# Linear attention with a gated feed-forward on one core: kv norm in three vector steps, q sums on ScalarE, k's block swap as a product, q0 in four pieces, leading products in K halves

## The chip, the core and the metric

The kernel runs on one core of one Trainium2 chip. The core has TensorE (PE, matrix products, results in PSUM), VectorE (DVE), ScalarE (ACT), GpSimd (POOL) and SyncE (SP, which here issues DMAs). The time is the device time of one execution in microseconds (us). Three executions of the kernel before gave 293.3 us (median; 292.95 to 293.79).

## The reference, cut to what matters

```python
def _attn_ref(q, k, v):                      # each (8, 8, 576, 64)
    q_s = np.exp(q - np.max(q, axis=-1, keepdims=True))
    q_s = q_s / (np.sum(q_s, axis=-1, keepdims=True) + 1e-09)
    k_s = np.exp(k - np.max(k, axis=2, keepdims=True))
    k_s = k_s / (np.sum(k_s, axis=2, keepdims=True) + 1e-09)
    kv = np.einsum('bhsd,bhse->bhde', k_s, v)
    return np.einsum('bhsd,bhde->bhse', q_s, kv)

x = attn_out.transpose(0, 2, 1, 3).reshape(4608, 512)
h = x @ w_in                                 # (512, 2048)
g = h * (1.0 / (1.0 + np.exp(-beta * h)))
out = g @ w_out                              # (2048, 512)
```

q is normalised along the 64 columns of a row, k along the 576 rows of a head. Inputs and output are float32; the kernel computes products in bfloat16 with float32 sums.

## The kernel before, in words

**Units.** The feed-forward works on 9 chunks of 512 tokens. Eight hold the first 512 tokens of a batch (8 of the 9 sub-rows i that a partition holds), and the chunk numbered 7 holds the last sub-row of all batches, the tails. The 2048 hidden columns are 16 blocks of 128. Unit n is chunk n // 16 and block n % 16, so there are 144 units. A unit goes through four operations, named in the order by letters:

- **h n** (`st1`, L510): four products over the K tiles of 128, into one PSUM bank hT of 128 x 512;
- **th n** (`tanh`, L524): ScalarE reads that bank and writes the tanh to SBUF;
- **g n** (`gate`, L533): VectorE computes (th + 1) * h from SBUF and that bank, so that h needs to be half of x @ w_in (the 2.0 in `kv_norm`);
- **o n** (`st2`, L554): four products of g with 128 rows of w_out into the four banks acc0 to acc3, which gather the 16 units of a chunk. After the sixteenth, `o_ev` copies each acc to SBUF (osb) and `store` writes it out.

**Rings.** PSUM has eight banks: four acc, and four tiles hT0 to hT3 that are dealt out in turn by `take` to h, but also to kv, x, xt and qtrt (below), to beta and to the fills. There are 8 buffers for g and 3 for th.

**Attention.** For batch b: `q_max` (VectorE, L226), `q_sub` (POOL, L238), `q_exp` (ScalarE, L243), `q_sum` and `q_rcp` (VectorE, L264, L271, L272), `q_norm` (POOL, L278), then a transpose qT: by DMA for b of 1 and more, by TensorE (`q_tr`, L298) with copies for batch 0. For k: `k_max` (VectorE, L315) gives maxima by blocks of 32 partitions; `k_small` (L332, L337, L340) reduces them, swaps neighbouring blocks of 32 partitions by four instructions of 32 x 8, and combines both with the sign turned; `k_rep` (L349) spreads the result, `k_sub` adds it (POOL or VectorE, L359), `k_exp` (L364) follows. `kv_mm` (L385) computes kv with the sum of k's exponentials as a 65th column, for two halves J of the heads; `kv_norm` (L400, L401, L403) divides by that column, five VectorE instructions a half. `x_mm` (L433) multiplies qT by kv into x, `x_ev` copies it to xT in SBUF; `xt_mm` (L466) does the same for the tails.

**Order.** The order of all operations is written out by name: the list FIRST (L17 to L69) up to batch 5, and after it by due times. Each engine runs its instructions in that order; waits between engines are set when the program is built, from the tiles that instructions read and write. Weights are loaded in 16 halves of 512 KB into four staging tiles and cast to bfloat16 on POOL, ScalarE or VectorE; a staging tile is loaded again after its cast. SP issues the loads in the order of the list, with at most eight on their way.

**The start.** Batch 0 is cut finer: q in sub-rows 0 to 3, 4 to 7 and 8, in two halves of heads; the first four units ("leading") in two halves of 256 tokens. `fill` (L644) runs products without use to keep TensorE occupied before there is work.

Of the kernel before, what the change touches and what calls it, by code (L numbers as in the profile page):

```python
# [13 lines left out]
EPS = 1e-9  # L14


FIRST = """  # L17
ld_q0_1, consts, ld_q0_0, ld_k0_0, ld_k0_1, ld_v0_0, ld_v0_1, ld_beta, ld_w0_0, ld_w0_1, ld_q1_1, ld_w2_0, ld_w1_0,
ld_w2_1, ld_q1_0, qmax_0_0_1, qmax_0_1_1, qmax_0_2_1, qsub_0_0_1, qsub_0_1_1, qmax_0_0_0, qsub_0_0_0, qexp_0_0_1,
qsum_0_0_1, qmax_0_1_0, qsub_0_2_1, qsub_0_1_0, kmax_0_0, qexp_0_1_1, qexp_0_0_0, vcast_0_0=pool, qsum_0_0_0,  # L20
kmax_0_1, qrcp_0_0, qnorm_0_0_0, qnorm_0_0_1, fill_0, qtr_0_0_0, fill_1, qtr_0_0_1, beta_tr, ksmall_0, krep_0_0,
krep_0_1, ksub_0_2, ksub_0_3, qexp_0_2_1, qexp_0_1_0, vcast_0_1, qtrev_0_0_0, kexp_0_2, cast_w0_1=pool, cast_w0_0,
ksub_0_1, ksub_0_0, qsum_0_1_0, qsum_0_1_1, qrcp_0_1, beta_ev, kexp_0_3, kexp_0_0, kexp_0_1, fill_2, kv_0_1,
qtrev_0_0_1, cast_w2_0=act, fill_3, kv_0_0, kvn_0_1, qnorm_0_1_1, ld_w1_1, ld_k1_0, ld_w4_0, ld_k1_1, ld_w4_1,
x_0_0_1, kvn_0_0, qnorm_0_1_0, x_0_0_0, qtr_0_1_1, qtr_0_1_0, ld_w3_0, xev_0_0_0, xev_0_0_1=act, h_0_0, h_3_0,
ld_w6_0, qtrev_0_1_1, th_0_0, qmax_1_2, qmax_1_3, qtrev_0_1_0=dve, qmax_0_2_0, qsum_0_2_1, g_0_0, x_0_1_1, x_0_1_0,
cast_w1_0=pool, qsub_0_2_0, cast_w2_1=pool, h_1_0, h_2_0, qexp_0_2_0, xev_0_1_0=dve, qsum_0_2_0, qrcp_0_2, qmax_1_1,
xev_0_1_1=act, h_0_1, th_1_0, th_3_0, th_0_1, h_1_1, h_2_1, h_3_1, g_0_1, th_1_1, g_1_0, g_1_1, qmax_1_0, qnorm_0_2_1,
qnorm_0_2_0, qsub_1_1, th_2_1, th_3_1, th_2_0, ld_w6_1, cast_w1_1=pool, qsub_1_0, cast_w4_1=pool, cast_w3_0, ld_w3_1,
ld_w5_0, ld_w7_0, ld_w5_1, ld_k2_0, ld_v1_0, ld_v1_1, ld_k2_1, h_4, th_4, kmax_1_0, kmax_1_1, g_2_0, g_2_1, g_4,  # L30
qexp_1_2, qexp_1_3, cast_w4_0, o_0_0, o_0_1, o_1_1, h_5, o_1_0, o_2_0, th_5, h_7, h_6, kmax_1_2, g_3_0, g_3_1,
kmax_1_3, o_3_0, g_5, h_8, o_2_1, o_3_1, o_4, h_9, qexp_1_1, qexp_1_0, th_7, th_6, ksmall_1, g_6, h_11, cast_w6_0,
th_8, krep_1, g_7, g_8, qsum_1_1, qsum_1_0, cast_w6_1, th_9, g_9, cast_w3_1=act, h_12, h_10, th_11, cast_w5_0,
ksub_1_0, qrcp_1_0, ld_w7_1, qnorm_1_0, qsum_1_2, qsum_1_3, g_11, qrcp_1_1, ksub_1_1=dve, qnorm_1_1, qT_1, ld_q2_1,
kexp_1_0, kexp_1_1, cast_w7_0, cast_w5_1=act, th_10, th_12, g_10, o_5, o_6, o_7, o_8, o_9, h_14, h_13, o_10, h_15,
kexp_1_2, kexp_1_3, th_14, th_13, vcast_1_0, vcast_1_1, cast_w7_1=pool, kmax_2_1, g_12, kmax_2_0, o_11, o_12, th_15,
g_14, g_13, g_15, kmax_2_2, kv_1_0, kv_1_1, o_13, o_14, kvn_1_0, kvn_1_1, kmax_2_3, x_1_0, xev_1_0, x_1_1, xev_1_1,
o_15, xev_1_2, xev_1_3=act, ksmall_2, qmax_2_3, qmax_2_2, h_16_0, h_16_1, h_28, h_17_0, h_17_1, oev_0_2, th_16,
oev_0_3=act, oev_0_1=act, th_17, oev_0_0, ld_q2_0, ld_v2_1, ld_k3_1, ld_v3_1, g_16, krep_2, qmax_2_0, st_0_0, ld_q3_1,
ld_v2_0, qsub_2_1, h_20, h_18, g_17, th_18, qmax_2_1, g_18, th_20, qexp_2_2, qexp_2_3, g_20, ksub_2_1, qsub_2_0,  # L40
vcast_2_1, ksub_2_0, vcast_2_0, qsum_2_2, kmax_3_2, o_16, h_24, o_17, h_21, kexp_2_2, th_21, g_21, h_19, th_19, g_19,
o_18, h_23, o_19, h_22, o_20, o_21, qexp_2_1, th_24, th_23, qexp_2_0, th_22, qsum_2_1, qmax_3_2, g_23, g_24, g_22,
qtrt_0, qsum_2_0, qsum_2_3, qrcp_2_0, qrcp_2_1, h_25, kexp_2_1, kexp_2_0, qtrtev_0_1, th_25, g_25, o_22, o_23, h_27,
kexp_2_3, th_28, th_27, h_26, o_24, o_25, qtrtev_0_0=dve, qmax_3_3, g_28, g_27, th_26, g_26, xt_0, kv_2_0, kv_2_1,
qnorm_2_0, qnorm_2_1, st_0_3, ld_k3_0, ld_q4_1, ld_q3_0, ld_v3_0, ld_k4_1, st_0_2, qT_2, ld_q4_0, ld_k4_0, qsub_3_1,
xtev_0_0, xtev_0_1, h_30, o_26, h_29, o_27, o_28, qexp_3_3, qexp_3_2, th_29, th_30, qmax_3_0, qmax_3_1, kmax_3_1,
kmax_3_3, kvn_2_0, kvn_2_1, qsum_3_3, g_29, x_2_0, xev_2_0, o_29, x_2_1, xev_2_1, xev_2_2, xev_2_3, h_31, th_31, h_32,
h_40, qsub_3_0, th_32, qsum_3_2, kmax_3_0, g_30, ksmall_3, krep_3, g_31, qmax_4_2, g_32, h_34, h_44, h_37, qexp_3_1,
th_34, g_34, th_37, qrcp_3_1, kmax_4_1, h_33, o_30, o_31, g_37, th_33, g_33, vcast_3_1=act, oev_1_0, oev_1_2, oev_1_3,
ld_q5_1, ld_v4_1, st_0_1, oev_1_1, kmax_4_2, h_36, th_36, g_36, h_35, o_32, o_33, qnorm_3_1, ksub_3_1, th_40, th_35,  # L50
g_40, kmax_4_3, g_35, qexp_3_0, qsum_3_1, o_34, h_39, th_39, g_39, h_38, th_38, g_38, qsum_3_0, qrcp_3_0, kmax_4_0,
h_42, h_41, ksub_3_0, vcast_3_0, kexp_3_1, kexp_3_3, th_41, h_43, o_35, o_36, o_37, o_38, st_1_0, st_1_1, ld_q5_0,
st_1_2, qnorm_3_0, g_41, th_42, th_43, th_44, g_42, g_44, g_43, ksmall_4, xt_1, krep_4, xtev_1_0=dve, h_46, h_45,
kexp_3_0, kexp_3_2, xtev_1_1, th_46, th_45, qmax_4_3, ksub_4_0, st_1_3, qT_3, ld_v4_0, ld_k5_0, ld_k5_1, qsub_4_1,
ksub_4_1, kexp_4_0, o_39, kv_3_0, kv_3_1, o_40, o_41, g_45, g_46, kvn_3_0, kvn_3_1, x_3_0, xev_3_0=dve, x_3_1, o_42,
xev_3_2, xev_3_1=dve, xev_3_3, h_48, th_48, h_49, qexp_4_3, qmax_4_1, g_48, qmax_4_0, qsub_4_0, vcast_4_1, h_51, h_52,
o_43, o_44, h_53, th_51, th_49, g_49, qexp_4_2, g_51, th_52, g_52, qsum_4_3, h_54, xt_3, th_54, o_45, xtev_3_0,
xtev_3_1, h_47, h_55, qexp_4_0, th_47, vcast_4_0=dve, g_47, th_55, kexp_4_1, o_46, o_47, g_54, kexp_4_2, g_55, h_50,
xt_2, oev_2_2, oev_2_0, xtev_2_1, th_50, oev_2_3, oev_2_1, o_48, st_2_1, g_50, qsum_4_2, o_49, st_2_2, h_56, th_53,
xtev_2_0, st_2_0, h_57, g_53, qrcp_4_1, th_56, qexp_4_1, o_50, st_2_3, th_57, g_56, qsum_4_0, qsum_4_1, o_51, ld_v5_0,  # L60
kexp_4_3, o_52, ld_v5_1, g_57, o_53, o_54, h_58, qmax_5_0, qrcp_4_0, qnorm_4_0=dve, qnorm_4_1, qmax_5_1, qT_4, o_55,
th_58, qsub_5_0, g_58, kv_4_0, h_59, kvn_4_0, qmax_5_2, o_56, th_59, qexp_5_0, g_59, kv_4_1, h_60, kvn_4_1, qmax_5_3,
o_57, th_60, qsub_5_1, g_60, x_4_0, xev_4_0, h_61, qsum_5_0, xev_4_1, o_58, qexp_5_1, x_4_1, th_61, h_62, xev_4_2,
g_61, xev_4_3, o_59, qsum_5_1, qexp_5_2, h_63, qrcp_5_0, th_62, qnorm_5_0, o_60, qexp_5_3, g_62, th_63, qsum_5_2,
h_64, g_63, o_61, th_64, qsum_5_3, h_65, qrcp_5_1, g_64, o_62, qnorm_5_1, th_65, kmax_5_0, h_66, g_65, o_63, kmax_5_1,
oev_3_0, vcast_5_0, qT_5, h_67, oev_3_2, oev_3_1, st_3_0, th_66, vcast_5_1, oev_3_3, o_64, th_67, g_66, st_3_1, h_68,
kmax_5_2, st_3_2, o_65, th_68, g_67, h_69, kmax_5_3, st_3_3, g_68, o_66, th_69, ld_q6_0, ksmall_5, h_70, ld_q6_1,
krep_5, g_69, ksub_5_0
"""  # L69
PLAN = {}  # L70
for _i, _t in enumerate(FIRST.replace("_", " ").split(",")):
    _n, _, _e = _t.strip().partition("=")
    PLAN[_n] = (_i - 10000, _e or None)


@with_exitstack
def kernel(
# [20 lines left out]
    NR = 4  # L98
    LAST = 8
    LAG = 3  # L100
    NG = 8
    TAILS = 7
    NCH = 9


    ops = []

    def at(when, name, fn, eng=None):
        if name in PLAN:
            when, eng = PLAN[name][0], PLAN[name][1] or eng  # L110
        ops.append((when, len(ops), name, fn if eng is None else lambda: fn(ENGINES[eng])))

    ENGINES = {"act": nc.scalar, "dve": nc.vector, "pool": nc.gpsimd}
# [8 lines left out]
    ident = sbt("ident", [P, P], BF16)  # L122
    warm = sbt("warm", [P, P], BF16)
    beta_rows = sbt("beta_rows", [NJ, P], F32)
# [15 lines left out]
    kneg = sbt("kneg", [P, KT, 2], F32)  # L140
# [5 lines left out]
    xT = [sbt(f"xT{i}", [P, KT, 512], BF16) for i in range(2)]  # L146
    xTt = sbt("xTt", [P, KT, 512], BF16)
    g = [sbt(f"g{i}", [P, 512], BF16) for i in range(NG)]
    th = [sbt(f"th{i}", [P, 512], BF16) for i in range(3)]
    osb = sbt("osb", [P, 4, 512], F32)  # L150

    ring = [ps.tile([P, 512], F32, name=f"hT{i}") for i in range(NR)]
    acc = [ps.tile([P, 512], F32, name=f"acc{i}") for i in range(4)]
    place = {}
    done = set()
    turns = [(f"free{i}", ring[i]) for i in range(NR)]
    done.update(w for w, _ in turns)

    def take(*who):

        assert sum(last in done for last, _ in turns) >= len(who)
        for w in who:
            n = next(n for n, (last, _) in enumerate(turns) if last in done)
# [86 lines left out]
    def zs_of(b):  # L250
        if b:
            return qz[:]
# [590 lines left out]
```

## Time and profile before

| what | value |
|---|---|
| median of three runs | 293.3 us |
| span of the profiled execution | 291.8 us |
| TensorE busy | 273.9 us (94%) |
| VectorE, ScalarE, GpSimd busy | 207.3, 173.2, 127.5 us |
| h products into hT (L510) of 128 x 512 | 379 ns each by the row, 0.865 us for four in a row |
| th, 128 x 512 (L524) | 689 ns x 140 |
| g, 128 x 512 (L533) | 680 ns x 140 |
| first h starts | 19.88 us |
| last product ends | 287.4 us |
| q, k or v load, 576 KB, issue to landing | 5.0, 7.1, 8.3 us (median) |

The profiled execution's own time isn't listed beside its span; the median of the runs lies 1.5 us above that span. A group's duration runs from the issue of an instruction to its end, and products overlap, so a row of them takes less than the sum of their durations: the distance from start to start counts. "Idle before" is the time that an engine stood still ahead of an instruction, with what ended it.

### The profile page before, as it was taken

The numbers are of one execution on the slowest core, as the hardware profiler recorded it, in microseconds if no ns is written. First come the engines' busy times: TensorE is split into PE (matmuls) and PEld (weight loads), VectorE is DVE, ScalarE is ACT, GpSimd is POOL, SyncE is SP. The second block draws the span as 40 slices with busy tenths as digits, with TensorE's granted clock in tenths as the row PEclk, the third lists the DMA queues.
The fourth block names the chain that finished last, engine by engine and source line by source line (L and its number), as shares of the span: only waits on it lengthen the run. The fifth ranks groups of instructions, "written<-read, shape, count | busy, mean of one in ns | idle before, by whom it ended". The sixth has DMA issues, their size and how long they took to land.

```text
span 291.8 us, 5151 instructions
## 1 busy us (share of the span) xinstructions
PE 273.9 (94%) x1891; PEld 124.2 (43%) x1922; DVE 207.3 (71%) x446; ACT 173.2 (59%) x292; POOL 127.5 (44%) x85
## 2 busy tenths in 40 slices
PE   0888999999999999999999999999999999999993
PEld 0345344444344444444444444444444444444441
DVE  3988999989978875897976798578834353345350
ACT  2588794985677656727537854775575454444450
POOL 4898485698347583233835373547350000000000
PEclk9999999999999999999999999999999999999999
DMA  7999999998956570392199109920900060006005
GB/s 263 383 393 388 379 388 227 391 350 291 232 211 148 148 258 1 91 244 56 38 212 396 67 12 223 372 109 0 222 5 3 0 142 4 0 0 145 2 12 131
DMA packets 39577, 50.61 MB, mean 173 GB/s; under 512 B 18544, under 2 KB 18560, under 8 KB 39552
## 3 DMA queue, kind: packets, MB, share of 16 engines
q1 hardware_dynamic: 39472, 50.15, 56.0%
q8 instruction: 15, 0.25, 0.4%
q10 hardware_dynamic: 80, 0.13, 0.1%
q14 instruction: 10, 0.08, 0.1%
HBM read 36.71 MB, written 9.44 MB: 158 GB/s over the span
## 4 chain that ended last, share of the span: by engine, by line
PE 79%; DMA 9%; DVE 3%; issue 3%; POOL 2%; ACT 1%; SPq 0%
PE hT L510 38%; PE acc L554 37%; DMA wst<-in_moe_w_in_dram 4%; DMA qT<-qn 4%; PE hT L433 2%; DMA qf<-in_q_dram 1%; PE hT L385 1%; POOL w_in_b L184 1%; ACT th L524 1%; DVE km L315 1%; DVE g L533 1%; POOL qf L238 1%; POOL kf L359 0%; PE hT L466 0%; DVE acc L264 0%
## 5 line engine op out<-in xcount | busy, mean ns | idle before, releaser
L554 PE MATMUL acc<-w_out_b,g 128*128 128x512 bf16 x567 | 141.6, 379 | 1.2 <-DVE osb L184 0.4
L533 DVE SCALAR_TENSOR_TENSOR g<-th,hT 128x512 bf16<-128x512 bf16 (+1 forms) x148 | 97.1, 665 | 63.0 <-ACT th L524 62.1
L524 ACT ACTIVATE th<-hT,beta_c 128x512 bf16<-128x512 f32 (+1 forms) x148 | 98.2, 677 | 71.6 <-PE hT L510 66.8
L510 PE MATMUL hT<-xT,w_in_b 128*128 128x512 bf16 (+1 forms) x508 | 124.8, 373 | 2.1 <-DVE g L533 0.7
L554 PEld LDWEIGHTS <-g 128*128 128x128 bf16 x576 | 55.6, 98 | 68.6 <-issue 1.9
L510 PEld LDWEIGHTS <-w_in_b 128*128 128x128 bf16 x592 | 55.8, 98 | 65.5 <-issue 4.0
L278 POOL TENSOR_TENSOR qn<-eq,qz 128x1152 bf16<-128x1152 bf16 (+2 forms) x19 | 33.5, 1770 | 37.7 <-DVE qz L272 33.2
L238 POOL TENSOR_TENSOR qf<-qf,qm 128x1152 f32<-128x1152 f32 (+2 forms) x20 | 34.4, 1732 | 26.8 <-DVE qm L226 20.4
L359 POOL TENSOR_TENSOR kf<-kf,kmb 128x1152 f32<-128x1152 f32 (+1 forms) x14 | 35.3, 2538 | 17.1 <-DVE kmb L349 17.1
L226 DVE TENSOR_REDUCE qm<-qf 128x9 f32<-128x576 f32 (+2 forms) x34 | 23.7, 708 | 5.8 <-DMA qf<-in_q_dram 5.7
L364 ACT ACTIVATE ek<-kf 128x576 bf16<-128x576 f32 x32 | 21.1, 683 | 7.7 <-POOL kf L359 7.7
L315 DVE TRANSPOSE_TENSOR_REDUCE km<-kf 128x18 f32<-128x576 f32 (+1 forms) x30 | 23.9, 802 | 0.5 <-DMA kf<-in_k_dram 0.5
L243 ACT ACTIVATE eq<-qf 128x576 bf16<-128x576 f32 (+2 forms) x34 | 21.8, 655 | 3.0 <-POOL qf L238 2.9
L264 DVE TENSOR_REDUCE qz<-eq 128x9 f32<-128x576 bf16 (+1 forms) x30 | 21.0, 712 | 0.0
L182 ACT CAST xT<-hT 128x512 bf16<-128x512 f32 x25 | 13.4, 589 | 9.1 <-PE hT L433 9.1
L182 ACT COPY osb<-acc 128x512 f32<-128x512 f32 x20 | 10.9, 590 | 12.1 <-PE acc L554 12.1
L510 PE MATMUL hT<-xTt,w_in_b 128*128 128x512 bf16 x62 | 16.2, 379 | 0.1
L184 POOL CAST va<-vf 128x1152 bf16<-128x1152 f32 x13 | 14.7, 1149 | 0.8 <-DMA vf<-in_v_dram 0.8
L644 PE MATMUL hT<-eq,warm 128*128 128x512 bf16 x23 | 7.5, 476 | 7.3 <-ACT eq L243 7.3
L184 DVE COPY osb<-acc 128x512 f32<-128x512 f32 x16 | 10.4, 687 | 5.3 <-PE acc L554 5.1
L385 PEld LDWEIGHTS <-ek 64*64 64x64 bf16 x576 | 6.0, 107 | 5.5 <-issue 2.5
L385 PE MATMUL hT<-va,ek 64*64 64x65 bf16 x576 | 7.6, 194 | 0.2 <-ACT ek L364 0.2
(55 smaller groups left out, 91.0 us busy)
## 6 DMA issues: line engine op xcount, KB each, us to landing
qf<-in_q_dram SPq DMA_DIRECT2D x16, 576.0 KB, 5.0
kf<-in_k_dram SPq DMA_DIRECT2D x16, 576.0 KB, 7.1
vf<-in_v_dram SPq DMA_DIRECT2D x16, 576.0 KB, 8.3
out_dram<-osb SPq DMA_DIRECT2D x71, 128.0 KB, 2.4
wst<-in_moe_w_in_dram SPq DMA_DIRECT2D x8, 512.0 KB, 10.5
wst<-in_moe_w_out_dram SPq DMA_DIRECT2D x8, 512.0 KB, 10.6
out_dram<-osb ACTq DMA_DIRECT2D x1, 128.0 KB, 2.6
qT<-qn SPq DMA_TRANSPOSE x7, 3.9
```

The source lines that it names most:

```text
L182: act.copy(dst, src)
L184: eng.tensor_copy(dst, src)
L226: dve.tensor_reduce(qm[:, j : j + n, i0:i1], qf[b % 2][:, j : j + n, i0:i1], axis=AX.X, op=ALU.max)
L238: eng.tensor_tensor(x, x, m, ALU.subtract)
L243: act.activation(eq[:, i0:i1, j : j + n, :].rearrange("p i j d -> p j i d"), qf[b % 2][:, j : j + n, i0:i1], ACTF.Exp,)
L278: eng.tensor_tensor(qn[b % 2][:, i0:i1, j : j + n, :], eq[:, i0:i1, j : j + n, :], z, ALU.mult)
L315: dve.tensor_reduce(km[:, j : j + n].rearrange("p j i e -> p (j i e)"), kf[b % 2][:, j : j + n].rearrange("p j i (e c) -> p (j i e) c", c=32),
L359: eng.tensor_tensor(x, x, m, ALU.add)
L510: pe.matmul(place[("h", n)][:, cols(h)], w_in_b[:, kt, u * P : (u + 1) * P], x[:, kt, cols(h)], start=(kt == 0), stop=(kt == KT - 1),)
L524: act.activation(th[n % 3][:, cols(h)], place[("h", n)][:, cols(h)], ACTF.Tanh, scale=beta_c[:, u : u + 1])
L533: dve.scalar_tensor_tensor(out=g[n % NG][:, cols(h)], in0=th[n % 3][:, cols(h)], scalar=1.0, in1=place[("h", n)][:, cols(h)], op0=ALU.add, ...
L554: pe.matmul(acc[t][:], g[n % NG][:, t * P : (t + 1) * P], w_out_b[:, u, :], start=(u == 0), stop=(u == NJ - 1),)
```

## The change

- **kv norm**: three VectorE instructions (add and double, reciprocal, multiply) over both banks, and for batches 1 to 7 over both halves J at once, after the second half of kv. To reach two banks in one instruction, the four tiles hT0 to hT3 become one tile hT of 128 x 4 x 512; `take_pair` gives kv two of its banks, and the halves lie 128 columns apart.
- **First q sums**: for batch 0, sub-rows 0 to 3, the exponential is done in 8 ScalarE instructions of 128 x 64 a half, each with its sum as a second output into acc2, in place of one instruction of 128 x 512 and a VectorE sum.
- **k's maximum**: for batch 0 the swap of blocks is one product with a permutation matrix, into a bank of hT; for others the four 32 x 8 copies stay. The maximum is kept with its own sign and subtracted.
- **eps** is added from a tile in `q_rcp`.
- **q0** is loaded in four pieces: sub-rows 0 to 3 and 4 to 8 of each half of heads.
- **Leading products**: each half unit's four K tiles are two operations, tiles 0 and 2, then 1 and 3.
- The constants eps and swap are made on POOL; the last copy of acc3 is shared between ScalarE and VectorE; the whole order is written out in one list ORDER, with the same operations in the same places, save that kv's norm of batches 4 to 7 stands after the second half and the new operations (kred, kswap) after beta's transpose.

```diff
-    ring = [ps.tile([P, 512], F32, name=f"hT{i}") for i in range(NR)]
+    ring = ps.tile([P, NR, 512], F32, name="hT")
...
     def take(*who):
         for w in who:
             n = next(n for n, (last, _) in enumerate(turns) if last in done)
+            i = turns.pop(n)[1]
+            place[w] = ring[:, i, :]
+            turns.append((w, i))
+    def take_pair(w):
+        free = [n for n, (last, _) in enumerate(turns) if last in done][:2]
+        a, b = sorted(turns[n][1] for n in free)
+        place[w] = ring[:, a : b + 1 : b - a, :]
...
-        for s in range(2):
-            dve.tensor_scalar(kz[:, s, J : J + 1], w[s][:, D : D + 1], EPS, 2.0, op0=ALU.add, op1=ALU.mult)
-        dve.reciprocal(kz[:, :, J], kz[:, :, J])
-        for s in range(2):
-            dve.tensor_tensor(kvn[b % 2][:, J, s, :], w[s][:, 0:D], ..., ALU.mult)
+        w = place[key][:, :, P * J0 : P * (J0 + n)].rearrange("p s (J c) -> p J s c", J=n)
+        dve.tensor_scalar(z, w[:, :, :, D], EPS, 2.0, op0=ALU.add, op1=ALU.mult)
+        dve.reciprocal(z, z)
+        dve.tensor_tensor(kvn[b % 2][:, J0 : J0 + n], w[:, :, :, 0:D], ..., ALU.mult)
...
+    def q_exp_sum(b, j, n, i0, i1):
+        for a in range(j, j + n):
+            for i in range(i0, i1):
+                act.activation(eq[:, i, a, :], qf[b % 2][:, a, i, :], ACTF.Exp,
+                    accum_out=acc[2][:, KT * i + a : KT * i + a + 1])
...
+    def k_swap(b):
+        take(("swap", b))
+        pe.matmul(place[("swap", b)][:, 0 : 2 * KT], swap[:],
+            kmr[:].rearrange("p j e -> p (j e)"), start=True, stop=True)
...
+    def k_small(b):
+        if b:
+            for a in range(4):
+                o = kmr[32 * (a ^ 1) : 32 * (a ^ 1) + 32]
+                dve.tensor_tensor(kms[32 * a : 32 * a + 32], o, o, ALU.max)
+        dve.tensor_tensor(kmx[:], kmr[:], other, ALU.max)
...
+    for J in range(2):
+        for h, (i0, i1) in enumerate(((0, 4), (4, NI))):
+            op(f"ld q0 {J} {h}", lambda J=J, i0=i0, i1=i1: load_q(0, 2 * J, i0, i1))
...
+            for h in range(2):
+                for x in range(2):
+                    op(f"h {n} {h} {x}", lambda n=n, h=h, x=x: st1(n, (x, x + 2), h))
...
+        if (c, t) == (NCH - 1, 3):
+            act.copy(osb[:, t, 0:256], acc[t][:, 0:256])
+            dve.tensor_copy(osb[:, t, 256:512], acc[t][:, 256:512])
```

## The prediction, as put on record before the result

> **What bounds the kernel now.** I read the page's busy shares first.
>
> ```profile
> span 291.8 us, 5151 instructions
> PE 273.9 (94%) x1891; PEld 124.2 (43%) x1922; DVE 207.3 (71%) x446; ACT 173.2 (59%) x292; POOL 127.5 (44%) x85
> ```
>
> TensorE is busy 94% of the span, so what it does and waits for sets the time. Next come its own waits in the view of waits, longest first:
>
> ```profile
> PE hT L644 <- ACT eq L243: 7.3, 1, 7.3
> PE acc L298 <- POOL qn L278: 1.1, 2, 1.0
> PE hT L510 <- DVE g L533: 0.7, 1, 0.7
> PE acc L554 <- DVE osb L184: 0.4, 1, 0.4
> PE hT L433 <- DMA qT<-qn: 0.4, 1, 0.4
> ```
>
> After the first 7.3 us nothing is over 1.1 us. Once the first products run, TensorE goes through almost without a gap to 287.4 us. Why it can is seen in the timeline of one unit late in the run (columns: start us, length us, engine, line, operation, operands, count, idle before):
>
> ```profile
> 243.00 1.03 PE L510 MATMUL hT<-xTt,w_in_b 128*128 128x512 bf16 x4
> 243.06 0.69 DVE L533 SCALAR_TENSOR_TENSOR g<-th,hT 128x512 bf16<-128x512 bf16 x1 [1.04 <-ACT th L524]
> 243.87 1.03 PE L554 MATMUL acc<-w_out_b,g 128*128 128x512 bf16 x4
> 244.07 0.69 ACT L524 ACTIVATE th<-hT,beta_c 128x512 bf16<-128x512 f32 x1 [1.04 <-PE hT L510]
> ...
> 244.73 1.03 PE L510 MATMUL hT<-xTt,w_in_b 128*128 128x512 bf16 x4
> 244.78 0.69 DVE L533 SCALAR_TENSOR_TENSOR g<-th,hT 128x512 bf16<-128x512 bf16 x1 [1.04 <-ACT th L524]
> ```
>
> A unit is h (four products into one bank of hT), th (ScalarE reads it), g (VectorE reads it), and an o of an older unit. h begins at 243.00, o at 243.87, the next h at 244.73: 0.865 us each, 1.73 a unit. The next h starts while g of the unit before has only just begun (244.78) and will end at 245.47. That overlap is the kernel's whole economy: four tiles, so h of unit n+1 waits for g of unit n-3.
>
> **The ring as one tile.** The change makes the four tiles hT0 to hT3 one tile of four banks, so that one VectorE instruction can reach two banks. Waits are placed when the program is built, so I compared the built instruction lists with their waits. In the changed one, h of unit 64 writes bank 3 and waits for g of unit 63, which reads bank 0; th of a later unit waits for a g of another bank; the copy of beta (bank 2) waits for the swap product (bank 3), and the third fill (bank 0) for the readers of both. In the list of before, h waits for the last reader of its own tile. So in the changed program all of hT is handed over as one thing: every access by one engine waits for the last access by another, in the order of the list.
>
> The price of a plain unit (h, its th, its g, then the next h) by rows: four products 0.86; from h's end to th's start 244.07 - 243.865 = 0.21, say 0.22 (a waited-for h at 25.16 gave its th at 26.27, 1.11 in all); th 0.69; 0.03 (244.76 to 244.78); g 0.68; and 0.05 from a g's end to a waiting product (g starts 24.70 and takes 0.41, the product starts 25.16). Sum 2.53 against 1.73: the o (0.86) fits into the 1.67 in which the others read, but 0.8 us of every unit is idle.
>
> Over the whole order I went through the list of operations and cut it into rounds: writes of hT by TensorE, then reads, until the next write. From the first h there are 137 rounds, and 63 are the plain form. Added up:
> - TensorE writing: 140 h x 0.864 = 121.0; the four leading units in halves 3.5; kv 7 x 1.4 (0.68 to 0.7 a pair); x 14 x 0.45; tails and the late transposes 2.6: 143.2. Second products o that stand between two writes of one round: 19.5. Together 162.7.
> - Reading, with a handover 0.22 + 0.05 a round, 0.03 per change of reader, 0.07 less for two reads in a row on one engine: 140 th x 0.69, 140 g x 0.68, halves 6.8, xev 28 x 0.6, xtev 16 x 0.26, kv norm 7 x 0.75: 259.7.
> - o's longer than the reads that cover them: 2.4.
> That is 424.8 us from the first h to the last. Before, the same stretch ran from 19.88 to 280.3, 260.4 us.
>
> In some rounds a reader stands on its engine behind other work that the cover (about 1.8 us a round) can't hold: a reciprocal step, two sums and four kexp or cast instructions between th of unit 11 and th of unit 10 (about 4.5), sums and the swap of k between the g of units 30 to 32 (1.6), between g 56 and 57 (1.5), before g 58 (1.5), smaller ones 4.4; and at five later chunk ends ScalarE's two copies of acc stand ahead of th, waiting for that chunk's last o (1.35 each, 6.8). Estimate 20 us; bounds 0 and 45 (if nothing hides, twice my list).
>
> **The start.** Q0 in four pieces: the first piece is 256 of 576 KB; at the 390 GB/s of the page's DMA row that is 0.84 us less than the 3.97 us to the first maximum. POOL's three new constants (rows 0.10, 0.20, 0.29) end before 3 us and are hidden by that transfer. Two more DMA issues (0.48 each) delay the queue behind by 1 us, but w0 still waits for landings. First sums on ScalarE: 16 instructions of 128x64 replace two of 128x512 (0.63) and two VectorE sums (0.69). The trace has none with a sum; a 128x16 copy took 0.16, the 128x128 exp 0.30, and each waits for the one before (0.03), so eight take 1.5 to 2.6; I take 2.2, nearer to the 0.30 row. ScalarE then has the sums at about 10.8, just as kmax ends (11.66 less the two sums), and POOL's v cast (to 11.90) holds the norm anyway: it gains 0.25 us there.
>
> The block swap: kms and kneg (12.13 to 13.03) go, and a product comes. But it stands on TensorE behind the transposes of both first qn halves:
>
> ```profile
> 13.06 0.39 DVE L349 STREAM_TRANSPOSE acc<-kneg 128x192 f32<-128x192 f32 x1
> ...
> 14.26 0.40 PE L298 MATMUL acc<-ident,qn 128*128 128x128 bf16 x4 [0.18 <-POOL qn L278]
> 14.59 0.23 PE L628 MATMUL hT<-ident_f,beta_rows 16*128 16x16 f32 x1
> ```
>
> The swap can't start before 14.8 - 0.25, takes about the 0.23 of the beta product, then max 0.15: krep at 15.1 instead of 13.06. Behind it wait VectorE's three ksub (2.08), ksub 3 and two weight casts on POOL, kexp and kv. So the first h comes at 19.88 + 1.7 = 21.6 (bounds: 0 if other waits of kv cover it, and 3).
>
> **Small parts.** kv norm for b of 1 to 7 becomes 3 steps (0.15 + 0.17 + about 0.4) for 10 (4 x 0.15 + 2 x 0.17 + 4 x 0.22 = 1.8); before, TensorE's own work hid it, now 0.75 stands in the sum. Adding eps by a tensor is one instruction for one. K halves: the same products in the order 0, 2, 1, 3; both xT copies are done before the first th, so I take nothing (bounds -0.6, one copy, and 0). The last copy is split over two engines: 0.59 becomes about 0.4, -0.2.
>
> **Sum.** 21.6 + 424.8 = 446.4; the last 32 o's 32 x 0.216 + 0.2 = 7.1: 453.5; the tail 291.8 - 287.4 - 0.2 = 4.2: 457.7; queues 20: 478. The median of the runs (293.3) lies 1.5 over the profiled span, so the time is **479 us**.
>
> **Rivals.**
> 1. *The clock.* TensorE falls idle 1.67 us in most rounds less an o, and up to 3.7 in some.
>
> ```profile
> 7.26 5.03 PE L644 MATMUL hT<-eq,warm 128*128 128x512 bf16 x14 [7.26 <-ACT eq L243]
> ```
>
> After 7.26 us without work the 128x512 product took 0.36 instead of 0.216, though the granted clock stands at full. If gaps keep it there, 162.7 grows by 0.67 of itself (109) and the last o's by 4.6: 592; half the time so, 535. Against it: at 20 to 25 us products kept 0.12 per 256 columns with gaps of 0.2 to 0.7. The Trainium skill (TensorE: Matmul & The Clock Gate, "What's actually happening") says the clock halves after an idle window of some 3.4 us and returns after a busy one; the 0.36 row agrees in kind. By it only two or three rounds here would pay, some 5 us in all.
> 2. *Queues cost nothing, or ScalarE and VectorE read different banks side by side.* The 20 us vanish, or foreign th and g overlap in the grouped rounds (some 25 us by the same rows): 454 to 459. The built waits speak against the second.
> 3. *Not slower.* h of unit n+1 does not in truth wait for g of unit n, the four banks turn as before, and only start and tail move. The start's +1.7 is absorbed in the idle that TensorE has from 20 to 32 us (0.22, 0.73, 0.30) because the weights whose cast ends at 32.09 land at 30.99 either way: 293.3 + 1.7 - 1.25 - 0.2 = 293.5. It decides where the next h starts: at g's beginning (244.73 against 244.78) or after its end (245.47). The Trainium skill (PSUM — Partial Sum Buffer, "PSUM bank collisions raise a hardware error") keeps engines apart only within one bank, so by it the chip needs no such wait, and the time would be this 293.5. Nothing in before's trace contradicts it, as it overlaps banks; but a wait in the program is obeyed whether the chip needs it or not.
>
> **Chances.** Forecast (460 to 510) 0.73; clock 0.12; 2: 0.12; 3: 0.03. The range 450 to 540 leaves out the third and most of the clock's case. A measurement of this kernel can tell about 0.3% (0.9 us) from no change: faster 0.01, same 0.02, slower 0.97.
>
> **What would show it.** TensorE near 57% busy; its longest wait by far h <- DVE g, some 0.8 us about a hundred times; h every 2.53 us late in the run; ScalarE's idle before th ended by PE, not g. krep near 15. An h that starts before g of the unit before has ended proves me wrong; products of 0.36 show the clock.

## The result, and the profile after

The changed kernel takes 508.7 us (median of four runs, 507.1 to 515.9) against 293.1 for the kernel before: 1.733 times as long, 95% interval 1.729 to 1.737. Here and below, medians are over all executions and ratios over those within 1.5% of the kernel's fastest. The forecast was 479, range 450 to 540. The page of the profiled execution begins so (busy us, share of the span, instructions; below it a row with the granted TensorE clock in tenths, 40 slices):

```profile
span 506.9 us, 5168 instructions
PE 330.9 (65%) x1924; PEld 134.8 (27%) x1924; DVE 203.2 (40%) x388; ACT 177.8 (35%) x322; POOL 128.0 (25%) x88
...
PEclk9789798889968897899999779987999689999969
```

Two things stand in it. TensorE is busy 65% instead of 94% of a longer span: it waits. And its busy time has grown from 273.9 to 330.9 us though its work is the same: its products are slower in places, and the clock row, full almost throughout before, dips below 9 in many slices. The same row of the kernel before:

```profile
PEclk9999999999999999999999999999999999999999
```

The view of TensorE's waits (us in total, times, longest) names the first cause:

```profile
PE hT L719 <- DVE g L746: 109.0, 87, 4.9
PE hT L719 <- ACT th L735: 14.8, 12, 3.1
PE hT L328 <- ACT eq L370: 8.4, 1, 8.4
PE hT L719 <- DVE kvn L548: 6.8, 3, 2.3
```

The line h <- g was 0.7 us once, and is now 109.0 us in 87 waits. The timeline of a late unit shows one of them (start us, length us, engine, line, operation, operands, count, idle before):

```profile
412.80 1.02 PE L719 MATMUL hT<-xTt,w_in_b 128*128 128x512 bf16 x4 [0.64 <-DVE g L746]
...
413.66 1.03 PE L767 MATMUL acc<-w_out_b,g 128*128 128x512 bf16 x4
413.86 0.69 ACT L735 ACTIVATE th<-hT,beta_c 128x512 bf16<-128x512 f32 x1 [1.83 <-PE hT L719]
...
414.58 0.69 DVE L746 SCALAR_TENSOR_TENSOR g<-th,hT 128x512 bf16<-128x512 bf16 x1 [1.83 <-ACT th L735]
415.32 1.02 PE L719 MATMUL hT<-xTt,w_in_b 128*128 128x512 bf16 x4 [0.64 <-DVE g L746]
```

From h to the next h it is 2.52 us, where it was 1.73. The next h no longer begins with the g of the unit before: it begins 0.05 us after that g's end (414.58 + 0.69 = 415.27).

The second cause shows when the busy time of each engine is asked for in consecutive stretches of 3.41 us. These are the steps in which the granted clock changes in this trace (columns: stretch, length, busy us and instructions of PE, PEld, DVE, ACT, POOL, granted clock, DMA share, GB/s):

```profile
389.87:393.28 3.41, 2.23 (x12) 0.89 (x12) 0.84 (x4) 0.12 (x1) 0.00 (x0) 1.00 0.00 0
393.28:396.69 3.41, 1.10 (x6) 0.51 (x6) 0.69 (x1) 1.54 (x3) 0.00 (x0) 1.00 0.03 5
396.69:400.11 3.42, 1.95 (x8) 0.47 (x7) 0.00 (x0) 1.42 (x3) 0.00 (x0) 0.51 0.00 0
...
403.52:406.93 3.41, 1.57 (x12) 0.54 (x11) 0.69 (x1) 1.01 (x3) 0.00 (x0) 0.50 0.00 0
406.93:410.35 3.42, 3.42 (x9) 1.18 (x8) 0.69 (x1) 0.69 (x1) 0.00 (x0) 0.50 0.00 0
410.35:413.76 3.41, 2.77 (x13) 1.17 (x12) 0.69 (x1) 0.69 (x1) 0.00 (x0) 0.99 0.00 0
```

Read each row's first busy figure with the next row's clock. 2.23 us of TensorE work is followed by a full clock, 1.10 by half, and the clock comes back after a stretch that was busy throughout (3.42). In the whole span 106.7 us are at half clock, in 19 spells. Every spell follows a stretch with at most 1.70 us of TensorE work. Where a stretch was busier than that, the full clock stayed. Between 1.37 and 1.70 us both happened. (The trace's record of the clock begins at 11.03 us.) In the kernel before, 0.8 us are at half clock, all after the last product.

Last, the start. The first h begins at 25.86 us (before 19.88, forecast 21.6):

```profile
15.89 0.23 PE L313 MATMUL hT<-ident_f,beta_rows 16*128 16x16 f32 x1
16.05 0.39 PE L456 MATMUL hT<-kmr,swap 128*128 128x8 f32 x2
18.68 2.29 PE L328 MATMUL hT<-eq,warm 128*128 128x512 bf16 x5 [2.25 <-ACT beta_c L317]
```

The swap product runs at 16.05, though VectorE had k's maximum reduced at 12.62. Then the third fill, which writes another bank of hT, waits 2.25 us for a copy of beta, and that copy stands on ScalarE behind an exponential of k that needed the late maximum.

### The profile page after: what moved, and what is told of

Same layout as the page of the kernel before. It is cut to its first block, busy times and chain, and to the rows that moved or that the text cites. A ratio compares the mean times of both kernels' runs of the same rounds, so it can differ in the third digit from the quotient of the medians.

```text
span 506.9 us, 5168 instructions
## 1 busy us (share of the span) xinstructions
PE 330.9 (65%) x1924; PEld 134.8 (27%) x1924; DVE 203.2 (40%) x388; ACT 177.8 (35%) x322; POOL 128.0 (25%) x88
## 4 chain that ended last, share of the span: by engine, by line
PE 43%; ACT 21%; DVE 21%; issue 4%; POOL 1%; ACTq 0%; DVEq 0%
PE hT L719 30%; DVE g L746 17%; ACT th L735 16%; PE acc L767 11%; ACT xT L221 2%; PE hT L576 1%; PE hT L528 1%; ACT osb L221 1%; DVE qz L380 1%; ACT ek L507 1%; ACT w_out_b L221 1%; DVE qm L339 1%; POOL kf L500 1%; DVE kvn L548 1%; DVE xT L223 0%
## 5 line engine op out<-in xcount | busy, mean ns | idle before, releaser
L719 PE MATMUL hT<-xT,w_in_b 128*128 128x512 bf16 (+1 forms) x528 | 150.9, 420 | 128.4 <-DVE g L746 98.3
L767 PE MATMUL acc<-w_out_b,g 128*128 128x512 bf16 x576 | 157.8, 408 | 2.5 <-DVE g L746 2.5
L719 PEld LDWEIGHTS <-w_in_b 128*128 128x128 bf16 x592 | 61.5, 104 | 231.9 <-issue 188.0
L767 PEld LDWEIGHTS <-g 128*128 128x128 bf16 x576 | 59.0, 104 | 81.8 <-issue 20.5
L380 DVE TENSOR_REDUCE qz<-eq 128x9 f32<-128x576 bf16 (+2 forms) x32 | 22.3, 711 | 0.0
L358 ACT ACTIVATE eq<-qf 128x576 bf16<-128x576 f32 (+2 forms) x32 | 20.4, 654 | 0.0
L576 PE MATMUL hT<-qT,kvn 64*64 64x512 bf16 x56 | 6.7, 464 | 5.3 <-DVE g L746 3.4
```

The source lines that it names most:

```text
L380: dve.tensor_reduce(qz[:, i0:i1, j : j + n], eq[:, i0:i1, j : j + n, :], axis=AX.X, op=ALU.add)
L719: pe.matmul(place[("h", n)][:, cols(h)], w_in_b[:, kt, u * P : (u + 1) * P], x[:, kt, cols(h)], start=(kt == 0), stop=(kt == KT - 1),)
L767: pe.matmul(acc[t][:], g[n % NG][:, t * P : (t + 1) * P], w_out_b[:, u, :], start=(u == 0), stop=(u == NJ - 1),)
```

## The experiments

Theory A is the prediction's: one tile is one thing to the waits set at building, so h n+1 waits for g n, and this makes the loss. The rivals are that the new work of the start makes it (S), or that the chip's clock makes it (C). The clock can also be a second term of A, brought by A's waits; e4 and e9 test that. Each kernel was compared with runs of the kernel before on the same chip (293.3 to 293.6 us).

**e1: four tiles again.** The ring of one-bank tiles comes back into the changed kernel; kv's normalisation then reads two tiles in five steps.

```diff
-    ring = ps.tile([P, NR, 512], F32, name="hT")
+    ring = [ps.tile([P, 512], F32, name=f"hT{i}") for i in range(NR)]
...
-        dve.tensor_scalar(z, w[:, :, :, D], EPS, 2.0, op0=ALU.add, op1=ALU.mult)
+        for s in range(2):
+            dve.tensor_scalar(z[:, :, s], w[s][:, :, D], EPS, 2.0, op0=ALU.add, op1=ALU.mult)
```

> The changed kernel with one edit: the ring is four tiles of one bank again, so the normalisation of kv reads two tiles and takes five VectorE steps in place of three. All else of the change (sums on ScalarE, the swap product, q0 in four pieces, halves of K) stays. Theory A (waits of the one tile make the loss): 294 to 300 us, of which up to 6 us is the later first layer product (25.86 us in the changed kernel against 19.88); the wait of hT for VectorE's g falls from 109 us to under 3 us, the granted clock is 1.00 throughout. Rival S (the new steps of the start, or the pieces of q0, make the loss): stays above 480. Rival C (the clock falls by itself, whatever the waits): granted clock stays near 0.9 and the time is near 320.

Measured 297.1 us, ratio 1.011 (1.008 to 1.014). The same page rows:

```profile
span 295.8 us, 5151 instructions
PE 276.8 (94%) x1893; PEld 126.3 (43%) x1924; DVE 202.5 (68%) x406; ACT 176.1 (60%) x322; POOL 128.0 (43%) x88
...
PEclk9986999999999999999999999999999999999998
```

The loss is gone, but for 3.6 us. No wait of h for g is left in the view of waits, and the clock row dips only in the start and in the last slice. All else of the change but the three-step normalisation is still in this kernel, so S falls as the cause of the 215 us, and C falls as a cause by itself: the low clock goes with the waits.

**e2: only the ring.** The kernel before, with its four tiles turned into the banks of one.

```diff
-    ring = [ps.tile([P, 512], F32, name=f"hT{i}") for i in range(NR)]
+    hT = ps.tile([P, NR, 512], F32, name="hT")
+    ring = [hT[:, i, :] for i in range(NR)]
```

> The kernel before with one edit: its four one-bank tiles of the ring become the four banks of one tile; nothing else of the change is in it. Theory A: 498 to 508 us (the changed kernel's 508.7 less what its later start costs, 4 to 6 us, more a little for the five steps of kv). By the terms of the prediction without any fall of the clock it would be near 475. Rival S: 293 to 296, since none of the new steps is there.

Measured 511.3 us, ratio 1.743 (1.738 to 1.749), 3 us above the expected range. These two lines alone make the loss:

```profile
PE hT L511 <- DVE g L534: 103.6, 84, 4.9
```

The 24 late units from the gate of unit 116 to that of 140 took 61.70 us here and 61.71 in the changed kernel; they took 40.58 in both the kernel before and e1.

**e3: two tiles of two banks.** kv keeps its three steps; h's alternate between the tiles.

```diff
-    ring = ps.tile([P, NR, 512], F32, name="hT")
+    ring = [ps.tile([P, 2, 512], F32, name=f"hT{i}") for i in range(2)]
...
-            n = next(n for n, (last, _) in enumerate(turns) if last in done)
+                i = next((i for i in free if (i[0] != mru[0]) != (w == ("h", 45))), free[0])
```

> The changed kernel with the ring as two tiles of two banks: kv's pair of banks is one tile, so its normalisation keeps the three steps, and the h's are dealt to the two tiles in turn. Theory A: h n+1 now waits for g n-1 instead of g n; by the late units g n-1 ends 1.62 us after h n-1, and the next h of that tile starts about 2.6 us after it at the full pace of 1.73 us a unit, so the wait costs nothing: the time of e1 within 2 us, 293 to 300. Rival H (any tile of more than one bank costs, in proportion to the banks it joins): about a third of the loss stays, 360 us or more.

Measured 351.6 us, ratio 1.195 (1.190 to 1.201). My expectation missed by 50 us, and the waits left are of the same kind:

```profile
PE hT L728 <- DVE g L755: 26.9, 33, 3.5
```

The gates tell where. The 24 late units took 40.83 us, as good as before, so the reasoning for a plain unit held. But up to unit 62 this kernel had lost 46.8 us on the kernel before (gate 62 at 185.1 against 138.3), 4.7 of them ahead of its first gate. There the hand-written order keeps three and four h's in flight (h 34, h 44 and h 37 in a row), and two of them always share a tile. I had reasoned from the late units alone. Rival H, a third of the loss per joined bank, gives a similar total but no such split.

**e12: one pair and two singles.** The start of e11 (below), kv of batches 1 to 7 in a tile of two banks, and h's on the two single banks first.

```diff
+    pair = ps.tile([P, 2, 512], F32, name="hTp")
+    ring = [ps.tile([P, 512], F32, name=f"hT{i}") for i in range(2)]
+    ring = [ring[0][:], ring[1][:], pair[:, 0, :], pair[:, 1, :]]
...
-            n = next(n for n, (last, _) in enumerate(turns) if last in done)
+            free = [n for n, (last, _) in enumerate(turns) if last in done]
+            n = next((n for n in free if (turns[n][1] < 2) != (w[:2] == ("xt", 1))), free[0])
```

> The kernel of e11 (start as before, 293.97 us) with the ring as two tiles of one bank and one tile of two: kv of batches 1 to 7 lies in the pair and is normalised in three steps, and the h's take the single banks first and the pair only where more than two are in flight. Theory A: in e3 the two tiles of two banks lost 54 us because the hand-written first half of the order keeps three and four h's in flight, and only 0.02 us a unit in the last 24 units; here the waits are left only for h's that share the pair, so a small part of that loss remains: 295 to 310. That three steps are worth anything by themselves would show as less than 293.3; theory A says they lie beside other work and do not. Rival H (each bank joined costs a third of the loss): 320 or more.

Measured 329.8 us, ratio 1.128 (1.124 to 1.133): another miss, and by its time the result that rival H asked for (320 or more). The waits by tile speak against H:

```profile
PE hT L741 <- DVE g L768: 17.5, 21, 2.0
...
PE hTp L741 <- DVE g L768: 2.1, 2, 1.5
```

The waits of h for g come to 2.1 us on the pair and to 17.5 on the single banks, which are not joined to anything. My rule dealt a single bank out again as soon as its g stood ahead in the order, instead of the bank that had rested longest, so h waited for a g that had only just been issued. That is a fault of the experiment, so it gives no verdict on the three steps. As in e3, the loss lies in the first half of the order: gate 62 comes at 166.1 us (138.3 before), while the 24 late units take 40.84 us. So the late units keep their 1.7 us each with this ring too; it is the dense first half of the order that loses by it.

**e4: fill the gaps of each unit.** Zero products behind each o of the changed kernel.

```diff
+        if u < NJ - 1 and n < NU - LAST:
+            for t in ts:
+                pe.matmul(acc[t][:], warm[:], w_out_b[:, u, :], start=False, stop=False)
```

> The changed kernel with more work: behind the four products of an o (all but the last o of a chunk and the last eight) four more are made with zero weights into the same banks, which adds nothing to the sums. They fill the 0.8 us in which TensorE stood idle in a late unit of 2.53 us. Theory A alone (the clock has no part): the unit becomes 0.86 + 1.73 = 2.59 us and the time rises by about 7 us, to 512 to 520. Theory A with the clock as its second term (the gaps make TensorE's clock fall, and this is the 30 us that the forecast of 479 lacked): the granted clock rises from 0.895 towards 1.00 and the time falls, though there are some 500 more products, to 480 to 495.

Measured 543.0 us (537.2 to 546.7), ratio 1.835 (1.828 to 1.841): both expectations fell. The profile is of the longest execution, 546.7 us, so the sizes that follow are that one's. TensorE was busy 422.0 us, 91 more than in the changed kernel, but its idle time from 25 us to its last product fell only from 157.6 to 104.5 us, by 53. The difference of 38 us is the added time: where several o's stand in a row, the extra ones find no gap. Much of the half clock stayed too (76 of 107 us), since it begins in long gaps ahead of an h that waits for kv or x, where there is no o. A test that aims at a gap has to put the work into that gap.

**e9: fill only the long gaps.** Six zero products behind each half of kv, each half of x, and the tails, for batches 4 to 7.

```diff
+    def zero(b):
+        if b > 3 and now[0] % NJ < NJ - 1:
+            for t in (0, 1, 2, 3, 0, 1):
+                pe.matmul(acc[t][:], warm[:], w_out_b[:, now[0] % NJ, :], start=False, stop=False)
```

> The changed kernel (one tile of four banks, 508.7 us) with 120 products of zero weights more, six behind each half of kv, each half of x and the tail products of batches 4 to 7, where TensorE stands idle for 1.4 to 2.5 us at a time; they add nothing to the sums. Theory A2 (the granted clock halves for the next 3.41 us where TensorE was busy for less than about 1.7 us of the last 3.41; the six products, 1.3 us, lift those windows over that): the 41 us of half clock between the gates 56 and 114 go, at 3.39 us a unit against 2.53 that is 10 us, and the products that find no gap cost up to 3 us: 498 to 504, and the stretch between these gates shrinks from about 199 us to about 190. Rival N (the half clock has no part in the time, or does not follow from the gaps): 508 to 514, and the stretch keeps 199 us or grows.

Measured 497.6 us, ratio 1.695 (1.690 to 1.701): 11 us less than the changed kernel, with 120 products more. In the stretch named, from gate 56 to gate 114, the time went from 199.1 to 190.1 us and the half clock from 41.0 to 0. First the changed kernel at x of batch 7, then the same place here:

```profile
398.00 0.64 PE L576 MATMUL hT<-qT,kvn 64*64 64x512 bf16 x4
401.12 1.86 PE L719 MATMUL hT<-xT,w_in_b 128*128 128x512 bf16 x4 [2.47 <-DVE g L746]
402.78 1.91 PE L767 MATMUL acc<-w_out_b,g 128*128 128x512 bf16 x4
```

```profile
392.56 0.41 PE L586 MATMUL hT<-qT,kvn 64*64 64x512 bf16 x4
392.90 1.47 PE L213 MATMUL acc<-w_out_b,warm 128*128 128x512 bf16 x6
395.44 1.02 PE L731 MATMUL hT<-xT,w_in_b 128*128 128x512 bf16 x4 [1.07 <-DVE g L758]
```

The wait for g is there in both. But with the gap filled, the four products of h take 1.02 us instead of 1.86. So the half clock follows from the gaps, and 41 us of it cost some 9 us, net of what the added products cost.

**e5 to e8: the start, part by part.** All on e1 (297.1 us). e5 puts the first sums back on VectorE, e6 replaces the swap product by four small copies, e7 loads q0 in two pieces, e8 does all three.

```diff
-                op(f"qexp 0 {h} {J}", lambda J=J, i0=i0, i1=i1: q_exp_sum(0, 2 * J, 2, i0, i1))
+            op(f"qexp 0 {h} {J}", lambda J=J, i0=i0, i1=i1: q_exp(0, 2 * J, 2, i0, i1))
...
-            other = place[("swap", b)][:, 0 : 2 * KT].rearrange("p (j e) -> p j e", j=KT)
+            dve.tensor_tensor(kms[32 * a : 32 * a + 32], o, o, ALU.max)
...
-ld_q0_1_0, ld_q0_1_1, consts, ld_q0_0_0, ld_q0_0_1,
+ld_q0_1, consts, ld_q0_0,
```

> The four-tile kernel (297.1 us) with the first sums of q0 back on VectorE: two Exp instructions and two reductions in place of sixteen Exp with accumulation. Theory P (the new work of the start is late because the swap product stands behind the fills on TensorE, and v0 lands late): in the four-tile kernel the sums end at 11.38 us and GpSimd's cast of v, ahead of q's normalisation there, ends at 12.8, so the sums are covered; 296.5 to 297.5. Rival Q (the sums on ScalarE make the start late, 2.8 us for eight): 294 to 295.

> The four-tile kernel with the block swap of k's maximum made by VectorE's four small operations, as for the other batches. Theory P: the maximum is reduced at 12.0 us and the swap product ran only at 15.4, after fourteen fills and eight transposes; VectorE idled 3.75 us. Without it k's maximum is spread at about 13.0 in place of 16.0, and what is late next is the cast of v on ScalarE (13.1 against 12.2) and q's normalisation on GpSimd (12.8 against 12.15): the first layer product comes 0.6 to 0.9 us later than in the kernel before; 294.0 to 294.8. Rival Q: 296.5 or more.

> The four-tile kernel with q0 loaded in two pieces as before. Theory P: v0's transfers start 1 us earlier, but the first q0 piece lands 1 us later, the sums end at 12.3 and the fills, which wait for the first of them, start at 9.4 and end near 15, so that the swap product is later still; 297 to 298. Rival R (the four pieces make the start late): 294 to 295.

> The four-tile kernel with all three undone: sums on VectorE, no swap product, q0 in two pieces. What is left of the change is the halves of K of the leading products and the order of kv's normalisation with both halves of heads together. Theory P: the time of the kernel before, 293.0 to 294.2. Rival K (the halves of K or the joined normalisation cost by themselves): 295 or more.

| kernel | median us | ratio to before (95%) |
|---|---|---|
| e5 | 296.9 | 1.013 (1.011 to 1.016) |
| e6 | 295.9 | 1.009 (1.007 to 1.011) |
| e7 | 297.4 | 1.013 (1.010 to 1.015) |
| e8 | 294.5 | 1.003 (1.002 to 1.004) |

The sums and the pieces each changed nothing beyond the spread, as expected. e6 and e8 gained, but less than expected. e6's timelines of VectorE and of GpSimd show why:

```profile
12.57 3.05 DVE L471 TENSOR_TENSOR kms<-kmr 32x8 f32<-32x8 f32 x4
```

```profile
13.37 2.06 POOL L398 TENSOR_TENSOR qn<-eq,qz 128x512 bf16<-128x512 bf16 x2
```

Four copies of 32 x 8 took 3.05 us instead of 0.69; singly 0.85, 1.00, 1.00 and 0.16. Each slow one ends within 0.02 us of the GpSimd instruction beside it. I had written the copies with two inputs in SBUF; the kernel before has one input, in PSUM.

**e10 and e11: copies from PSUM.** e10 is e6 and e11 is e8 with k's first maximum in a PSUM bank and one-input copies.

```diff
+        return acc[2][:, 64 : 64 + 2 * KT].rearrange("p (j e) -> p j e", j=KT)
...
-                dve.tensor_tensor(kms[32 * a : 32 * a + 32], o, o, ALU.max)
+                dve.tensor_scalar(kms[32 * a : 32 * a + 32], o, 1.0, None, op0=ALU.mult)
```

> The four-tile kernel without the swap product, k's first maximum reduced into a PSUM bank and its blocks exchanged by four one-input copies from there, as the kernel before does. In e6 three of the four two-input copies took 1.0 us each, just as long as GpSimd's normalisation of q beside them. Theory L (an operation of VectorE with two inputs in SBUF waits for the GpSimd operation that runs): the copies take 0.7 us again, k's maximum is spread at about 13.2 in place of 15.9, and the kernel takes 294.0 to 294.8. Rival: copies still slow, 295.9 as in e6.

> The four-tile kernel with sums on VectorE, no swap product, q0 in two pieces, and the copies from PSUM as in e10. Theory L: the 1.1 us that e8 lost against the kernel before go; 293.0 to 293.9, no difference from the kernel before that can be measured. Rival K (the halves of K or the joined normalisation cost): 294.3 to 294.7, as e8.

Measured 294.8 us, ratio 1.005 (1.003 to 1.007), and 294.0 us, ratio 1.0025 (1.001 to 1.004). e11 lies between its two expectations, and its interval excludes a ratio of 1. In e10:

```profile
13.18 0.69 DVE L481 TENSOR_SCALAR kms<-acc 32x8 f32<-32x8 f32 x4
```

0.69 us again. The Trainium skill (SBUF — State Buffer, "Who interferes with whom") states that a VectorE instruction with two inputs in SBUF contends with a GpSimd instruction that reads SBUF, and calls the port pair that they share an exclusive lock; 3.05 against 0.69 us agrees. e10 changed two things, the second input and the place of the first, and does not separate them: in the kernel before, a copy with a single input in SBUF also took 0.96 us beside a GpSimd cast (at 32.50 us).

So the swap product's part of what e1 lost is 2.3 us (297.1 to 294.8), and that of sums and pieces together 0.8 (to 294.0). Part of the 2.3 may be clock and not the product's own time: the mean granted clock was 0.985 to 0.999 in e1's executions and 0.995 to 1.000 in e10's, and e1's fastest, at 0.999, took 295.3 us. The last 0.6 us, of e11 against the kernel before (293.3 us on that chip), I did not place; the joined normalisation, the halves of K and the other small parts of the change are in it.

## Why the prediction was right, and where its terms were off

**The ring** held: the loss is the handover of the whole tile, shown alone in e2 and taken away in e1. Rival 3 falls: from unit 114 on, every h starts 0.05 us after the end of g of the unit before.

**The plain unit**: 2.53 us forecast, 2.52 measured.

**The start**: first h at 21.6 forecast, 25.86 measured, outside my bounds of 19.9 to 22.9. I gave it one term, the swap behind the transposes (krep at 15.1; measured 16.67). With four tiles (e1) the first h comes at 22.88, so new work costs 3.0 us there, and with the one tile the two together cost 6.0. The one tile alone costs 0.8 (e2: first h at 20.71). So most of the second 3.0 us arises where the two meet: the whole-tile waits, the fill's 2.25 us above all, then hang on the late maximum of k. I had put 1.7 us for the new work and nothing for whole-tile waits before the first h. Half clock has a part in it (five fills take 2.29 us, in e1 1.24), but it is not shown to follow from the waits: e5, with four tiles, has the 2.29 as well. Eight sums on ScalarE took 2.8 us and not 2.2: an Exp of 0.26 and a read of the accumulator of 0.15 in steps of 0.35; they were covered, as e5 shows. I had the DMA queue 1 us late, but not v0 with it: its issue comes at 3.79 us instead of 2.80 and GpSimd's cast of it at 12.34 instead of 10.75, and with the cast q's norm and the transposes ahead of the swap are late.

**The clock** is the term that was mis-sized. I set it at nothing in the sum, with 592 and 535 as a rival and some 5 us beside it by the Trainium skill's rule. Half clock came in 106.7 us of the span, 95.6 of them between the first spell, which ends at 28.1 us, and the last product. At e9's price, 9.07 us for 41.0 (0.22 us for each), that is an estimated 21 us. The Trainium skill (TensorE: Matmul & The Clock Gate, "What's actually happening") has a free-running window of 3413 ns and lets the clock fall after an idle one. The grid of 3.41 us here agrees, but half-idle windows sufficed: I had counted only rounds with a gap as long as a window. Rival 1 also misread its row: the 14 products are not at 0.36 us each with a full clock. They start 0.43 us apart up to 11.05 us and 0.22 after it, and the trace's record of the clock begins, at full, at 11.04 us; ahead of it the page prints full for want of a record.

**The sum**: 479 forecast, 508.7 measured. Start +4.3 and the estimated clock +21 are 25 of the 30 us. For the queues, which I gave 20 us (0 to 45), there remain 24: the span 506.9 less the first h at 25.86, 424.8 of rounds, 21 of clock and 11.1 from the last g to the end. That is a remainder; no run measures the queues, nor the 424.8 by itself.

**Small parts**: the three-step normalisation shows no gain on the whole time. In the joined ring it may have one: from gate 56 to gate 114, where batches 4 to 7 are normalised, e2 with its ten steps a batch takes 206.4 us and the changed kernel 199.1, but e2 has 13.6 us more of half clock there, and the two are not separated. TensorE was busy 65% and not 57%, since slow products count as busy. The waits of h for g were 87 of 1.25 us on average, not a hundred of 0.8, because the long ones at kv and x are among them.

## What to carry to other kernels

Before joining PSUM banks into one tile to save an instruction, write down who waits for whom on the joined tile: where waits are kept by tile, the depth of the ring is lost, and here two lines (e2) cost 218 us. When TensorE gets gaps, add the clock to the sum: look at how busy it is in each 3.41 us, not for one long gap. And read an order at its densest place, not only at its plainest unit: e3's expectation held for the plain unit and was wrong by 50 us over the whole.

## What the runs showed of the hardware that was not expected

- In the traces of the changed kernel, e2, e3, e4 and e9 the granted clock changes only on a grid of 3.41 us and only between full and half. It fell after stretches of 3.41 us with at most 1.93 us of TensorE work, and came back after stretches with at least 2.61.
- More work can shorten a run: 120 useless products in the gaps took 11 us off, 9 of them in the stretch where the half clock went (e9).
- A 32 x 8 copy on VectorE with both inputs in SBUF took 1.00 us beside GpSimd's normalisation (e6); with its one input in PSUM it took 0.15 to 0.17 (e10).
- An Exp with a sum over 64 columns costs ScalarE 0.35 us a step, of which a separate read of the accumulator shows as 0.15.
